# A fused routed-attention and MLP kernel on one core: one pool of eight accumulator banks, 512-column exponentials, steps ordered by a wanted time, weights from the first exponential on, unread matmuls in planned gaps

## The chip, the core and the metric

The kernel runs on one core of a Trainium2 chip. The metric is the time of one launch in device microseconds (us); the figure to beat is the median of three runs. One further execution is profiled, and the traces that are quoted come from that one. The engines are PE (matmuls and transposes; PEld is its weight load), ACT (exponentials, tanh, copies), DVE and POOL (vector work) and SP, which here only issues DMAs. "PEclk" is the TensorE clock that was granted, as a share of full speed.

## The reference

```python
# q, k, v: 4 x 8 x 768 x 64 (batch, head, row, dim); 16 centroids of 64 for each head
q_assign = argmax(q_n . c_n);  k_assign = argmax(k_n . c_n)      # nearest centroid, all normalized
scores = q . k^T / 8, and -1e9 where q_assign != k_assign
attn = softmax(scores);  x = (attn . v), heads side by side      # x: 3072 x 512
h = x @ w_in                                                     # w_in: 512 x 2048
out = (h / (1 + exp(-h))) @ w_out                                # w_out: 2048 x 512
```

Everything comes in and goes out as float32. The mask is made a part of the matmul: each row of q and k gets 16 more numbers, a code of its centroid, so that the 80-row product of a q and a k of different centroids is pushed far down.

## The kernel before

**Tiles.** A batch has 768 rows, which are 6 tiles of 128. A *part* (function `part`) prepares q and k rows of one head or a pair of heads: split float32 into two float16 halves (`hi` L436 or L432, `lo` L440), transpose them (DMA transpose L453, or PE transposes L467 with a copy out of the bank L476/L478), multiply by the centroids (`logits`, L505, or L496 with L500), find the maximum (L532), compare with it (L535, L556, L558), turn the code by 32 x 32 blocks (L565) and place it below the transposed rows in the tile `ab` (four `put`s: DMAs L578, or copies L580 and L582). `attention` then does one head: scores into a bank (L621), the exponential (L634) into the tiles `P`, the product with v (L653), reciprocal and scaling (L666, L671), and for each pair of heads the transpose of the result into `xt` (DMA L690, or PE L701 with copy L708). `mlp` takes a chunk of rows: 16 up blocks of 4 matmuls (L730), tanh (L736), gate (L741), then for each 128 rows 16 down matmuls (L759), a copy out (L772) and the store (L777).

**Stages.** Batch 0 is attended in two goes: first its row tiles 0 and 1 of all 8 heads (called n=0 below), then tiles 2 to 5 (n=1). Then come batches 1, 2 and 3, here b1, b2, b3. The MLP has eight chunks: batch 0 rows 0:2, batch 0 rows 2:6, then two chunks of 3 tiles for each other batch. The prepared rows of batch 0 that n=0 needs go over PE transposes and copies (`twin=True`, `place="ENG"`); the q rows that only n=1 needs, and all of b1 to b3, go over DMA transposes and DMA puts.

**Order.** Nothing is scheduled while the kernel runs: each engine executes a fixed list in order and waits in place. The lists come from `Plan.order`, a planner that is run while the kernel is built: it holds every step with an engine, an assumed duration, the steps that it follows and the buffers that it needs, and always takes the step that can start earliest by its own clock; at equal times the lower `key` wins. Loads and parts of later heads also follow the first exponential of an earlier head (`todo`, `pace`): the first loads of b1 that of head 1 of n=1, in both kernels. Buffers (tiles and PSUM banks) come from pools. The keys before are hand-written numbers: attention head places times 20, MLP steps from 100000 up, and some large negative ones for what should go at once.

**PSUM.** Eight banks of 512 columns: two pairs `pS` for scores only (an exponential reads 768 or 1024 columns of a pair at once), and four single banks `pM` for all else. `exps[-1].adds` gives the four score banks to the second pool after the last exponential.

**Weights.** w_in and w_out come in eight pieces each by POOL's DMA queue (`weight`, L791 and L795). Each step first copies one column of an exponential's result (L789), so that it can't run before that exponential: piece n of w_in hangs on exponential 8 + 2n, piece n of w_out on 26 + 2n, counted over the whole kernel.

**Warm-up.** 60 matmuls of zeros (L278) at the lowest priority keep PE busy before the first real one.

Of the kernel before, what the change touches and what calls it, by code (L numbers as in the profile page):

```python
# [33 lines left out]
class Plan:  # L34
# [33 lines left out]
    def order(self):  # L68
# [12 lines left out]
        done = 0  # L81
        while done < len(self.steps):
            best = None
            for e in engines.values():
# [60 lines left out]
        return sorted(self.steps, key=lambda s: (s.start, s.n))  # L145

@with_exitstack
def kernel(
# [35 lines left out]
    def many(name, n, shape, dt):  # L184
# [21 lines left out]
        "P": (12, [128, 128 * max(NJ, 2 * NB)], f16),  # L206
# [39 lines left out]
    W_IN, W_OUT = 8, 26  # L246
    WARM = 60
    LATE = 1000


    def consts_v():
        nc.vector.memset(zeros, 0.0)
# [21 lines left out]
    def warm(last):  # L274
        y = buf("M")

        def f():
            nc.tensor.matmul(banks[y.i][:, 0:256], zeros[:, 0:128], zeros, start=True, stop=True)  # L278

        return step("PE", 112, f, after=[s_const, last], use=[y], key=1e9, lag=0)  # L280

    last = None
    for _ in range(WARM):
        last = warm(last)
# [41 lines left out]
    def load_v(b, p, key, pace=None):  # L326
# [6 lines left out]
        for h in range(2):  # L333
# [9 lines left out]
            cast_v[b, 2 * p + h] = step("POOL", pool_w(384), g, after=[s, s_ones], use=[x, y], key=key + 60)  # L343
# [47 lines left out]
    def part(b, p, segs, a0, key, hi_eng="POOL", turn="DMA", twin=False, sub="POOL", place="DMA", code_eng=None, pace=None):  # L391

        n = sum(j1 - j0 for _, _, j0, j1 in segs)
# [18 lines left out]
        for kind, h, j0, j1, t, hs in merged:  # L412
# [34 lines left out]
            los.append(step("DVE", dve_w(64 * m, 1.25), lo, after=[x, lds], use=[nat, hl], key=key + 0.1))  # L447

        if turn == "DMA":
# [5 lines left out]
            turned = [step("SP", 120 * n, turn_dma, after=[his, los], use=[hl, A], key=key + 0.5, load=195 * n, flip=True, slack=LATE)]  # L455
        else:
            turned = []
            for kind, h, j0, j1, t, hs in merged:
# [49 lines left out]
        s_log = step("PE", SMALL * n * (2 if twin else 1), logits, after=[turned, s_cent], use=[A, Lb], key=key + 1)  # L508
# [395 lines left out]
```

## Time and profile before

| | before |
|---|---|
| median of 3 runs | 346.21 us (345.95 to 349.98) |
| the profiled execution | 343.36 us, of which its span is 341.5 us |
| PE busy | 310.4 us of the span (91%), mean granted clock 0.95 |
| ACT busy | 224.3 us (66%) |
| DVE busy | 199.0 us (58%) |
| POOL busy | 80.0 us (23%) |
| moved by DMA | 43.88 MB |

The profiled execution has 1.86 us around its span. The median run is 2.85 us above the profiled execution. Busy shares are means over stages that differ much, so the stages are what to read.

### The profile page before, as it was taken

The numbers are of one execution on the slowest core, as the hardware profiler recorded it, in microseconds if no ns is written. First come the engines' busy times: TensorE is split into PE (matmuls) and PEld (weight loads), VectorE is DVE, ScalarE is ACT, GpSimd is POOL, SyncE is SP. The second block draws the span as 40 slices with busy tenths as digits, with TensorE's granted clock in tenths as the row PEclk, the third lists the DMA queues.
The fourth block names the chain that finished last, engine by engine and source line by source line (L and its number), as shares of the span: only waits on it lengthen the run. The fifth ranks groups of instructions, "written<-read, shape, count | busy, mean of one in ns | idle before, by whom it ended". The sixth has DMA issues, their size and how long they took to land.

```text
span 341.5 us, 7888 instructions
## 1 busy us (share of the span) xinstructions
PE 310.4 (91%) x3035; PEld 189.6 (56%) x3035; DVE 199.0 (58%) x467; ACT 224.3 (66%) x359; POOL 80.0 (23%) x168
## 2 busy tenths in 40 slices
PE   8779587796999999979999989999999999989995
PEld 7667454543355555546665656656765564544542
DVE  5988753445465757476975579468873163261430
ACT  4687488563299877687877878768976863351431
POOL 3723441572130233313212214223100000000000
PEclk9955999659899999999999999999999999999999
DMA  7535969999965969888274975996061200101001
GB/s 227 192 111 93 161 94 177 239 166 143 222 127 133 197 135 170 217 203 219 45 136 90 228 192 88 238 209 143 11 121 42 86 2 31 61 2 61 32 30 65
DMA packets 97174, 43.88 MB, mean 128 GB/s; under 512 B 74608, under 2 KB 94064, under 8 KB 97136
## 3 DMA queue, kind: packets, MB, share of 16 engines
q1 hardware_dynamic: 90448, 39.08, 51.6%
q0 software_dynamic: 6400, 4.20, 9.8%
q8 instruction: 24, 0.39, 0.5%
q10 hardware_dynamic: 288, 0.10, 0.1%
q14 instruction: 14, 0.11, 0.1%
HBM read 27.30 MB, written 6.29 MB: 98 GB/s over the span
## 4 chain that ended last, share of the span: by engine, by line
PE 67%; DMA 14%; DVE 6%; ACT 4%; issue 4%; SPq 3%; POOL 1%; ACTq 0%; DVEq 0%; POOLq 0%
PE pM L759 19%; PE pM L730 16%; PE pS L621 14%; DMA ab<-hl 9%; PE pM L653 8%; DMA ab<-ohT 4%; PE pS L730 4%; ACT P L634 2%; SPq L578 2%; PE pS L759 2%; PE pM L505 2%; ACT tn L736 2%; DMA nk<-in_k_dram 2%; PE pM L278 2%; DVE hl L440 1%
## 5 line engine op out<-in xcount | busy, mean ns | idle before, releaser
L634 ACT ACTIVATE P<-pS 128x768 f16<-128x768 f32 (+1 forms) x184 | 149.0, 844 | 43.8 <-PE pS L621 40.4
L621 PE MATMUL pS<-ab 80*128 80x512 f16 (+1 forms) x384 | 90.9, 347 | 8.7 <-DMA ab<-ohT 4.1
L759 PE MATMUL pM<-wout_s,gq 128*128 128x512 f16 x352 | 86.3, 384 | 0.0
L730 PE MATMUL pM<-xt,win_s 128*128 128x384 f16 (+2 forms) x428 | 81.6, 329 | 4.3 <-DMA win_s<-in_moe_w_in_dram 3.7
L741 DVE SCALAR_TENSOR_TENSOR gq<-tn,pM 128x384 f16<-128x384 f32 (+2 forms) x107 | 56.5, 547 | 33.8 <-ACT tn L736 32.6
L730 PEld LDWEIGHTS <-win_s 128*128 128x128 f16 x512 | 49.1, 97 | 42.7 <-issue 5.4
L736 ACT ACTIVATE tn<-pM 128x384 f32<-128x384 f32 (+2 forms) x107 | 51.9, 504 | 20.6 <-PE pM L730 19.6
L759 PEld LDWEIGHTS <-gq 128*128 128x128 f16 x384 | 37.3, 98 | 41.1 <-issue 2.8
L621 PEld LDWEIGHTS <-ab 80*128 80x128 f16 x384 | 35.9, 102 | 34.8 <-issue 12.5
L653 PEld LDWEIGHTS <-P 128*128 128x128 f16 x1152 | 43.9, 102 | 10.5 <-ACT P L634 3.2
L653 PE MATMUL pM<-vt,P 128*128 128x65 f16 x1116 | 45.4, 200 | 2.5 <-ACT P L634 2.1
L535 POOL TENSOR_TENSOR Df<-L,mx 128x192 f32<-128x192 f32 (+1 forms) x28 | 15.1, 541 | 81.5 <-DVE mx L532 80.2
L338 POOL CAST vt<-nv 128x384 f16<-128x384 f32 x32 | 16.6, 543 | 54.4 <-DMA nv<-in_v_dram 32.6
L666 DVE RECIPROCAL rz<-pM 128x6 f32<-128x6 f32 (+2 forms) x39 | 7.1, 182 | 35.3 <-PE pM L653 35.0
L772 ACT COPY ot<-pM 128x512 f32<-128x512 f32 x22 | 12.9, 588 | 22.1 <-PE pM L759 21.4
L741 DVE SCALAR_TENSOR_TENSOR gq<-tn,pS 128x384 f16<-128x384 f32 x21 | 11.6, 554 | 19.6 <-ACT tn L736 16.0
L521 DVE TENSOR_REDUCE L<-pM 128x192 f32<-128x384 f32 (+1 forms) x28 | 14.9, 533 | 13.9 <-PE pM L505 11.3
L440 DVE SCALAR_TENSOR_TENSOR hl<-nq,hl 128x384 f16<-128x384 f32 (+3 forms) x33 | 19.4, 587 | 5.5 <-POOL hl L436 4.4
L440 DVE SCALAR_TENSOR_TENSOR hl<-nk,hl 128x384 f16<-128x384 f32 (+1 forms) x29 | 19.4, 667 | 4.6 <-POOL hl L436 4.6
L736 ACT ACTIVATE tn<-pS 128x384 f32<-128x384 f32 x21 | 9.9, 489 | 14.4 <-DVE gq L741 8.4
L671 DVE TENSOR_TENSOR xn<-pM,rz 128x384 f16<-128x384 f32 (+2 forms) x39 | 18.5, 475 | 1.2
L565 DVE STREAM_TRANSPOSE ohT<-oh 128x384 f16<-128x384 f16 (+2 forms) x33 | 18.6, 565 | 1.0
(59 smaller groups left out, 206.8 us busy)
## 6 DMA issues: line engine op xcount, KB each, us to landing
nv<-in_v_dram SPq DMA_DIRECT2D x16, 384.0 KB, 5.2
out_dram<-ot SPq DMA_DIRECT2D x24, 256.0 KB, 2.2
nk<-in_k_dram SPq DMA_DIRECT2D x15, 384.0 KB, 4.7
nq<-in_q_dram SPq DMA_DIRECT2D x12, 384.0 KB, 4.7
win_s<-in_moe_w_in_dram POOLq DMA_DIRECT2D x8, 256.0 KB, 4.9
wout_s<-in_moe_w_out_dram POOLq DMA_DIRECT2D x8, 256.0 KB, 8.6
ab<-ohT SPq DMA_DIRECT2D x96, 12.0 KB, 1.9
nq<-in_q_dram SPq DMA_DIRECT2D x4, 256.0 KB, 3.9
```

What stands on the lines that cost most here:

```text
L338: nc.gpsimd.tensor_copy(T["vt"][y.i][:, 0 : NJ * VW].rearrange("p (j c) -> p j c", c=VW)[:, :, 0:D], T["nv"][x.i][:, h, :].rearrange("p (j ...
L440: nc.vector.scalar_tensor_tensor(out=dl, in0=src, scalar=QS, in1=dh, op0=ALU.mult, op1=ALU.subtract)
L535: (nc.gpsimd if sub == "POOL" else nc.vector).tensor_tensor(out=T["Df"][Df.i][:, 0:n, :], in0=Lv(), in1=T["mx"][mx.i][:, 0:n].unsqueeze(2) ...
L565: nc.vector.transpose(T["ohT"][ohT.i][:, 0:n, :].rearrange("p n c -> p (n c)"), T["oh"][oh.i][:, 0:n, :].rearrange("p n c -> p (n c)"),)
L621: nc.tensor.matmul(pS[sb.i][:, at : at + 128 * (c1 - c0)], ab[0:80, kt[per * s + i], :], ab[0:80, qt + c0 : qt + c1, :].rearrange("p n c - ...
L634: nc.scalar.activation(out=dst, in_=src, func=AF.Exp, bias=0.0, scale=ESC)
L653: nc.tensor.matmul(banks[O.i][:, (D + 1) * t : (D + 1) * t + nn], w, vt[:, VW * j : VW * j + nn], start=(j == 0), stop=(j == NJ - 1), skip ...
L671: nc.vector.tensor_tensor(out=T["xn"][xn.i][:, 0:nq, (h % 2) * D : (h % 2) * D + D], in0=banks[O.i][:, 0 : (D + 1) * nq].rearrange("p (t c ...
L730: nc.tensor.matmul(banks[bank.i][:, 0:n], win_s[:, r, ts(fb, 128)], T["xt"][xtb[b].i][:, r, 128 * j0 : 128 * j1], start=(r == 0), stop=(r ...
L736: nc.scalar.activation(out=T["tn"][tn.i][:, 0:n], in_=banks[bank.i][:, 0:n], func=AF.Tanh, bias=0.0, scale=1.0)
L741: nc.vector.scalar_tensor_tensor(out=T["gq"][g.i][:, fb % 4, 0:n], in0=T["tn"][tn.i][:, 0:n], scalar=1.0, in1=banks[bank.i][:, 0:n], op0=A ...
L759: nc.tensor.matmul(banks[bank.i], T["gq"][gqs[quarter].i][:, fc % 4, ts(t, 128)], wout_s[:, fc, :], start=(fc == 0), stop=(fc == NFB - 1),)
```

## The change

One pool of eight banks serves all PSUM users, and every exponential reads one bank of 512 columns: for two k tiles of a full head that is 4 q tiles of the first, 4 of the second, and the last 2 of both together (9 exponentials for a head in place of 6 of 768 columns; n=1: 6 of 512 in place of 3 of 1024; n=0: 3 of 512 in place of 2 of 768; 288 in all in place of 184). The matmuls of the scores stay as they were. There are 20 tiles `P` of 512 columns in place of 12 of 1024. Keys become wanted times in us: the table `AT` gives when n=0, n=1, b1, b2, b3 should begin, `ML` when each MLP chunk should, and every step gets a key around that. The down matmuls are planned 2 at a time in place of 4. The weight pieces hang on exponentials 0 to 7 (w_in) and 10 to 17 (w_out), all of them in n=0. The q rows for n=1 go over PE, ACT and DVE (`**engines`) in place of DMA. The 60 warm-up matmuls go; in their place the planner puts an unread matmul of zeros (L284 of the changed kernel) into each gap of over 112 ns that it foresees on PE in its first 80 us while a bank is free. 140 of them come of it: 76 stand ahead of the first scores of n=0, 58 inside n=0 (12 of them right behind its first scores, 44 in its last third), and six later.

```diff
     def order(self):
+            if s.eng == "PE" and self.filler:
+                pool, w, make, until = self.filler
+                while t - e["t"] > w and e["t"] < until and pool.free and pool.free[0][0] <= e["t"]:
+                    x = Step()
+                    x.eng, x.w, x.fn, x.start, x.key, x.n = "PE", w, make(pool.free[0][1]), e["t"], 1e9, s.n - 0.5
...
+                    extra.append(x)
...
-        "P": (12, [128, 128 * max(NJ, 2 * NB)], f16),
+        "P": (20, [128, 512], f16),
...
-    pS = [ps.tile([128, 1024], f32, name=f"pS{i}") for i in range(2)]
-    pM = [ps.tile([128, 512], f32, name=f"pM{i}") for i in range(4)]
-    pools |= {"S": Pool(2), "M": Pool(4)}
+    banks = [ps.tile([128, 512], f32, name=f"bank{i}") for i in range(8)]
+    pools["M"] = Pool(8)
...
-    W_IN, W_OUT = 8, 26
-    WARM = 60
+    W_IN, W_OUT = 0, 10
+    UNREAD = 80000.0
+    AT = [12, 33, 63, 119, 186, 253]
+    ML = [36, 64, 122, 156, 188, 222, 255, 276, 297]
+    FINE = 2
...
-    def part(b, p, segs, a0, key, hi_eng="POOL", turn="DMA", twin=False, sub="POOL", place="DMA", code_eng=None, pace=None):
+    def part(b, p, segs, a0, due, lead=20.0, hi_eng="POOL", turn="DMA", twin=False, sub="POOL", place="DMA", code_eng=None, pace=None):
+        key = due - lead
...
-    def attention(b, h, j0, j1, key, turn):
+    def attention(b, h, j0, j1, key, per, turn):
-        per = {6: 1, 4: 2, 3: 2, 2: 3}[nq]
+        if nq == 6:
+            units = []
+            for j in range(0, NJ, 2):
+                units += [[(j, 0, 4)], [(j + 1, 0, 4)], [(j, 4, 6), (j + 1, 4, 6)]]
+        elif nq == 2:
+            units = [[(j, 0, 2), (j + 1, 0, 2)] for j in range(0, NJ, 2)]
+        else:
+            units = [[(j, 0, nq)] for j in range(NJ)]
...
-    def mlp(b, j0, j1, base, evac):
+    def mlp(b, j0, j1, t0, t1, evac):
-            kk = 100000 + base + fb
+            kk = t0 + (t1 - t0) * fb * 4.0 * n / whole
...
             lambda s, p=p: part(
-                0, p, [("q", 0, NA, NJ), ("q", 1, NA, NJ)], 2 * (NJ + NA), 40 + 20 * p, hi_eng="POOL", pace=s
+                0, p, [("q", 0, NA, NJ), ("q", 1, NA, NJ)], 2 * (NJ + NA), want[1, 2 * p], lead=15.0, pace=s,
+                turn={"q": "ACT"}, code_eng=["DVE", "DVE", "DVE", "ACT"], **engines,
             ),
...
-        w_in_done.append(weight("in", n, exps[W_IN + 2 * n]))
-        w_out_done.append(weight("out", n, exps[W_OUT + 2 * n]))
-    exps[-1].adds = (pools["M"], [4, 5, 6, 7])
+        w_in_done.append(weight("in", n, exps[W_IN + n]))
+        w_out_done.append(weight("out", n, exps[W_OUT + n]))
```

The changed order at three places. First POOL's list where the weights are issued (L789 or L804 is the wait for an exponential, `hl<-nq` the first step of the q rows for n=1). Before, one stretch of it:

```order
L436 TENSOR_SCALAR hl_86<-nq_81 128x8x64
L789 CAST pace<-P_112 128x1
L791 DMA win_s<-in_moe_w_in_dram 128x4x256
L436 TENSOR_SCALAR hl_87<-nq_82 128x8x64
L789 CAST pace<-P_114 128x1
L791 DMA win_s<-in_moe_w_in_dram 128x4x256
L535 TENSOR_TENSOR Df_134<-L_129,mx_132 128x128
L789 CAST pace<-P_104 128x1
```

In the changed kernel, the end of one unbroken row of 16 weight issues and what follows it:

```order
L804 CAST pace<-P_121 128x1
L810 DMA wout_s<-in_moe_w_out_dram 128x2x512
L442 TENSOR_SCALAR hl_88<-nq_80 128x8x64
L442 TENSOR_SCALAR hl_86<-nq_81 128x8x64
L442 TENSOR_SCALAR hl_87<-nq_82 128x8x64
L442 TENSOR_SCALAR hl_88<-nq_83 128x8x64
L342 CAST vt_102<-nv_84 128x6x64
```

All 16 pieces now stand ahead of the four splits for n=1, where before the two kinds alternated. Next SP's list between the q loads for n=1 and the first loads for b1 (`nk_78` with 128x2x384). Before:

```order
L316 DMA nq_82<-in_q_dram 128x2x256
L453 DMA_TRANSPOSE ab_89<-hl_88 128x8x128
L316 DMA nq_83<-in_q_dram 128x2x256
L453 DMA_TRANSPOSE ab_90<-hl_86 128x8x128
L578 DMA ab_89<-ohT_139 16x8x32 x4
L453 DMA_TRANSPOSE ab_91<-hl_87 128x8x128
L453 DMA_TRANSPOSE ab_92<-hl_88 128x8x128
L578 DMA ab_90<-ohT_137 16x8x32 x4
L578 DMA ab_91<-ohT_138 16x8x32 x4
L301 DMA nk_78<-in_k_dram 128x2x384
L578 DMA ab_92<-ohT_139 16x8x32 x4
```

In the changed kernel:

```order
L320 DMA nq_81<-in_q_dram 128x2x256
L320 DMA nq_82<-in_q_dram 128x2x256
L320 DMA nq_83<-in_q_dram 128x2x256
L305 DMA nk_78<-in_k_dram 128x2x384
L320 DMA nq_80<-in_q_dram 128x2x384
L334 DMA nv_84<-in_v_dram 128x2x384
L702 DMA_TRANSPOSE xt_131<-xn_135 128x4x128
L305 DMA nk_79<-in_k_dram 128x2x384
```

The four transposes and 16 puts of n=1 have left SP's list, and the loads of b1 follow at once. Last ACT's list where n=0 ends and n=1 begins (`P` exponentials, `tn` tanh of the first MLP chunk). Before:

```order
L634 ACTIVATE P_107<-pS_149 128x768
L736 ACTIVATE tn_140<-pM_153 128x256
L736 ACTIVATE tn_141<-pM_151 128x256
L736 ACTIVATE tn_142<-pM_152 128x256
L736 ACTIVATE tn_140<-pM_150 128x256
L634 ACTIVATE P_108<-pS_148 128x1024
```

In the changed kernel:

```order
L644 ACTIVATE P_106<-bank_162 128x512
L749 ACTIVATE tn_148<-bank_162 128x256
L749 ACTIVATE tn_149<-bank_161 128x256
L482 COPY ab_89<-bank_160 128x1024
L482 COPY ab_90<-bank_156 128x1024
L749 ACTIVATE tn_150<-bank_159 128x256
L749 ACTIVATE tn_148<-bank_163 128x256
L749 ACTIVATE tn_149<-bank_158 128x256
L482 COPY ab_91<-bank_162 128x1024
L586 COPY ab_89<-ohT_147 16x8x32
L482 COPY ab_92<-bank_157 128x1024
L644 ACTIVATE P_113<-bank_161 128x512
```

Four copies of 1024 columns and the first of four code copies, which the DMAs did before, now stand on ACT ahead of n=1's first exponential.

More of the change, by code (lines that the diff above doesn't have):

```diff
@@ L144, in order @@
             done += 1
-        return sorted(self.steps, key=lambda s: (s.start, s.n))
+        return sorted(self.steps + extra, key=lambda s: (s.start, s.n))
 @with_exitstack
@@ L255, in consts_v @@
         nc.vector.memset(stk, 0.0)
-    s_const = step("DVE", 900, consts_v, key=-100)
+    step("PE", 1, lambda: None, after=[step("DVE", 220, lambda: nc.vector.memset(zeros, 0.0), key=-101)], key=-100)
+    s_const = step("DVE", 700, consts_v, key=-100)
     def consts_p():
@@ L271, with unread @@
     s_ones = [v_ones(i) for i in range(sizes["vt"][0])]
-    def warm(last):
-        y = buf("M")
+    def unread(i):
         def f():
[L278 to L284, printed above, removed]
+            nc.tensor.matmul(banks[i][:, 0:256], zeros[:, 0:128], zeros, start=True, stop=True)
+        return f
+    plan.filler = (pools["M"], 112.0, unread, UNREAD)
     nks, nqs, nvs = {}, {}, {}
@@ L446, in part @@
             his.append(x)
-            los.append(step("DVE", dve_w(64 * m, 1.25), lo, after=[x, lds], use=[nat, hl], key=key + 0.1))
+            los.append(step("DVE", dve_w(64 * m, 1.25), lo, after=[x, lds], use=[nat, hl], key=key + span))
         if turn == "DMA":
@@ L453, in turn_dma @@
                 nc.sync.dma_start_transpose(T["ab"][A.i][:, a0 : a0 + n, :], src)
-            turned = [step("SP", 120 * n, turn_dma, after=[his, los], use=[hl, A], key=key + 0.5, load=195 * n, flip=True, slack=LATE)]
+            turned = [step("SP", 120 * n, turn_dma, after=[his, los], use=[hl, A], key=key + 2 * span, load=195 * n, flip=True, slack=LATE)]
         else:
@@ L506, in logits @@
                     t += 1
-        s_log = step("PE", SMALL * n * (2 if twin else 1), logits, after=[turned, s_cent], use=[A, Lb], key=key + 1)
+        s_log = step("PE", SMALL * n * (2 if twin else 1), logits, after=[turned, s_cent], use=[A, Lb], key=key + 8 * span)
         mx, Df, oh, ohT = buf("mx"), buf("Df"), buf("oh"), buf("ohT")
@@ L527, in Lv @@
                 return T["L"][Lu.i][:, 0:n, :]
-            top = [step("DVE", dve_w(32 * n), total, after=[s_log], use=[Lb, Lu], key=key + 1.2)]
+            top = [step("DVE", dve_w(32 * n), total, after=[s_log], use=[Lb, Lu], key=key + 9 * span)]
         def peak():
@@ L538, in below @@
             )
-        x = step("DVE", dve_w(16 * n), peak, after=top, use=[Lu, mx], key=key + 1.3)
-        s_below = step(sub, pool_w(16 * n, 2.7) if sub == "POOL" else dve_w(16 * n), below, after=[x], use=[Lu, mx, Df], key=key + 1.4)
+        x = step("DVE", dve_w(16 * n), peak, after=top, use=[Lu, mx], key=key + 10 * span)
+        s_below = step(sub, pool_w(16 * n, 2.7) if sub == "POOL" else dve_w(16 * n), below, after=[x], use=[Lu, mx, Df], key=key + 10.5 * span)
         marks = []
@@ L560, in part @@
             marks.append(
[L561 removed]
+                step("DVE", dve_w(16 * (t1_ - t0_), 0.65, 170), mark, after=[s_below, s_const], use=[Df, oh], key=key + 11 * span)
             )
@@ L568, in flip @@
             )
-        s_flip = step("DVE", dve_w(32 * n, 1.04, 180), flip, after=marks, use=[oh, ohT], key=key + 1.6)
+        s_flip = step("DVE", dve_w(32 * n, 1.04, 180), flip, after=marks, use=[oh, ohT], key=key + 12 * span)
         placed = []
@@ L779, in store @@
                 )
-            x = step(eng, act_w(512) if eng == "ACT" else dve_w(512), leave, after=[last], use=[bank, ot], key=-500)
-            step("SP", ISSUE, store, after=[x], use=[ot], key=-500, load=760)
+            x = step(eng, act_w(512) if eng == "ACT" else dve_w(512), leave, after=[last], use=[bank, ot], key=kk - 3)
+            step("SP", ISSUE, store, after=[x], use=[ot], key=kk - 3, load=760)
     def weight(kind, n, x):
```

163 lines of the change are left out of this document (84 added, 79 removed).

## The prediction

> **What bounds the kernel now.** I read the page's shares first, then the 40 slices, then busy time by stage, then the chain.
>
> ```profile
> PE 310.4 (91%) x3035; PEld 189.6 (56%) x3035; DVE 199.0 (58%) x467; ACT 224.3 (66%) x359; POOL 80.0 (23%) x168
> PEclk9955999659899999999999999999999999999999
> DMA  7535969999965969888274975996061200101001
> ```
>
> PE is the busiest by far, but its clock and the DMA share change after slice 10 (85 us). So I cut the span where the program's stages change: the first exponential (16.00), the first up matmul (38.97), the up matmuls of chunk 0, 2:6 (85.84), the first scores of b1 (about 94.5), the end of attention, the last matmul. The last four rows are the stretches at half clock and the window ahead of the first. Columns are busy us of PE, PEld, DVE, ACT, POOL, then the granted clock and the DMA share.
>
> ```profile
> 0.00:16.00 16.00, 13.35 (x175) 11.34 (x175) 11.81 (x36) 7.93 (x15) 9.64 (x30) 1.00 0.66 208
> 16.00:38.97 22.97, 18.89 (x247) 14.96 (x247) 19.25 (x56) 18.11 (x25) 8.23 (x15) 0.63 0.59 120
> 38.97:85.84 46.87, 36.10 (x384) 22.54 (x380) 23.42 (x64) 28.61 (x40) 18.93 (x39) 0.85 1.18 165
> 85.84:94.50 8.66, 8.07 (x31) 3.21 (x30) 4.21 (x9) 2.56 (x5) 1.47 (x3) 0.82 0.97 205
> 94.50:276.00 181.50, 175.42 (x1870) 107.22 (x1868) 117.93 (x262) 143.43 (x227) 41.77 (x81) 1.00 0.65 142
> 276.00:337.80 61.80, 58.53 (x342) 30.33 (x339) 22.34 (x44) 23.09 (x49) 0.00 (x0) 1.00 0.09 35
> 337.80:341.50 3.70, 0.00 (x0) 0.00 (x0) 0.00 (x0) 0.58 (x1) 0.00 (x0) 1.00 0.19 73
> 13.94:17.35 3.41, 2.70 (x52) 2.19 (x52) 3.20 (x8) 3.11 (x6) 2.00 (x5) 1.00 0.37 113
> 17.35:34.42 17.07, 15.20 (x195) 12.46 (x195) 14.37 (x41) 14.38 (x21) 5.21 (x10) 0.50 0.41 96
> 61.73:75.38 13.65, 12.76 (x94) 6.84 (x93) 6.86 (x16) 9.26 (x11) 9.39 (x19) 0.50 1.29 219
> 85.62:89.03 3.41, 3.41 (x17) 1.19 (x14) 1.68 (x5) 0.60 (x1) 0.51 (x1) 0.50 1.14 305
> ```
>
> From 94.5 to 337.8 PE is idle for only 243.3 - 175.42 - 58.53 = 9.4 us, at full clock: nothing but less work for PE could shorten that much. Ahead of it is the slack: between 38.97 and 85.84 (n=1) PE is busy 36.10 of 46.87 us at 0.85 clock, some 30.7 us of work, and DMA is overcommitted at 1.18. The chain names what ended n=1:
>
> ```profile
> 72.78 12.54 DMA ab<-hl
> 85.31 0.05 issue
> 85.36 0.48 PE pM L505 x12
> 85.84 1.71 PE pM L730 x4
> 327.42 10.37 PE pM L759 x48
> ```
>
> A transpose for b1 landed 12.54 us late, PE stood in order behind it, and from 85.84 the rest runs to 327.42 + 10.37 = 337.79. So the time is **T**, where chunk 0, 2:6 starts, plus a nearly full PE list. I work out T, then the list.
>
> **Up to the end of n=0.** The price of a 512-column exponential isn't in the trace; its neighbours are:
>
> ```profile
> L634 ACT ACTIVATE P<-pS 128x768 f16<-128x768 f32 x160 | 125.1, 817 | 34.4 <-PE pS L621 34.1
> L634 ACT ACTIVATE P<-pS 128x1024 f16<-128x1024 f32 x24 | 24.0, 1024 | 9.4 <-PE pS L621 6.3 <-POOL hl L436 2.9
> L772 ACT COPY ot<-pM 128x512 f32<-128x512 f32 x22 | 12.9, 588 | 22.1 <-PE pM L759 21.4 <-ACT P L634 0.5
> 78.57 1.94 ACT L634 ACTIVATE P<-pS 128x1024 f16<-128x1024 f32 x2 [0.94 <-PE pS L621]
> L278 PE MATMUL pM<-zeros 128*128 128x256 f16 x60 | 8.4, 303 | 1.0 <-DVE zeros L252 1.0
> ```
>
> 256 columns more cost 207 ns, so 512 cost 817 - 207 = 610 alone (the copy of that shape: 588). Two in a row take 1.94 in place of 2.05, so about 0.10 is saved when ACT isn't waiting: 0.51 to 0.61, and I take 0.56. n=0 gets 24 of them for 16 of 768: 24 x 0.610 - 16 x 0.817 = +1.6 us on ACT, which is busy 18.11 of 22.97 there. Unread matmuls: 76 now stand ahead of the first scores (60 before) and 12 right behind; at 8.4 / 60 = 0.14 each that is 28 more, up to 3.9 us. PE idles 16.00 - 13.35 = 2.65 us there, which hides most; but eight of them stand ahead of the centroids' transpose (42 in place of 34), and those I count in full: +1.1. The 44 in n=0's last third fall where ACT and DVE set the pace. Against that, PE ran at half clock from 17.35 to 34.42 and was busy 15.20 of 17.07: there it held ACT up. With the clock kept, I return 2.7 of ACT's 4.9 idle us, so the three cancel and the first up matmul stays at **39.0**. Bounds: -4.9 (all of ACT's idle time) to +5.5 (1.6 + 3.9). The 16 weight pieces hide beside this on POOL, which is busy only 8.23 of 22.97; were they late, the q splits behind them would be, and n=1 with them.
>
> **n=0 to n=1.** The q rows for n=1 now take engines: a DVE `lo`, 8 PE transposes, an ACT copy of 1024, 16 logits, three short DVE steps, the block transpose, three copies.
>
> ```profile
> L440 DVE SCALAR_TENSOR_TENSOR hl<-nq,hl 128x512 f16<-128x512 f32 x4 | 2.7, 686 | 0.1
> L476 ACT COPY ab<-pM 128x1024 f16<-128x1024 f16 x3 | 3.0, 1015 | 1.1 <-PE pM L467 1.1
> L535 DVE TENSOR_TENSOR Df<-pM,mx 128x128 f32<-128x128 f32 x2 | 0.6, 292 | 0.1
> L565 DVE STREAM_TRANSPOSE ohT<-oh 128x256 f16<-128x256 f16 x6 | 2.7, 444 | 0.2
> L582 DVE COPY ab<-ohT 16x256 f16<-16x256 f16 x4 | 1.6, 389 | 0.2
> 43.39 1.02 ACT L634 ACTIVATE P<-pS 128x1024 f16<-128x1024 f32 x1 [2.09 <-PE pS L621]
> ```
>
> 0.69 + 1.02 + 3 x 0.29 + 0.44 + 3 x 0.39 = 4.2, with about 1.5 of PE and hand-overs 5.7: n=1's first exponential at 44.7, 1.3 later than the 43.39 of before. Bounds 43.4 (it hides beside n=0's end) to 47 (the first two parts in a row on DVE).
>
> **n=1.** Up to the last n=1 exponential ACT's list holds 48 exponentials of 512, 11 tanh, 3 code copies and 2 copies of 512.
>
> ```profile
> L736 ACT ACTIVATE tn<-pM 128x256 f32<-128x256 f32 x16 | 6.0, 387 | 5.2 <-PE pM L730 4.8
> L580 ACT COPY ab<-ohT 16x256 f16<-16x256 f16 x4 | 1.6, 401 | 1.5 <-DVE ohT L565 1.5
> 83.01 0.42 DVE L708 COPY xt<-pM 128x512 f16<-128x512 f16 x1
> ```
>
> 48 x 0.56 + 11 x 0.39 + 3 x 0.40 + 2 x 0.59 = 33.6: the last one ends at 78.3. PE's 30.7 us and 16 down matmuls more (3.5) fit beside it. Bounds: 0.51 each gives 75.9, 0.61 gives 80.7. Then the last product with v, reciprocal, scaling, transposes and copy (before, from 78.57 + 1.94 = 80.51 to 83.01 + 0.42 = 83.43, so 2.9): 2.1 with less on DVE's queue, so **T = 80.4**.
>
> This needs b1's parts in time. Before, they were late because everything wanted DMA at once:
>
> ```profile
> 42.43 7.81 SPq L578 DMA_DIRECT2D ab<-ohT  x8
> 50.28 0.59 SPq L301 DMA_DIRECT2D nk<-in_k_dram  x1
> 96.21 0.75 POOL L795 DMA_DIRECT2D wout_s<-in_moe_w_out_dram  x1 [0.27 <-issue]
> q0 software_dynamic: 6400, 4.20, 9.8%
> ```
>
> Eight puts for n=1 held SP's queue until 50.24 (7.81 us), b1's first load went at 50.28, and the last weight piece was issued at 96.21. q0, the weights, takes 9.8% of 341.5 = 33.5 us of all 16 engines, 2.1 us a piece. Twelve pieces of 16 lay in n=1 and after, 25 us; DMA's 1.18 x 46.87 = 55.3 us of work there falls to about 30, 0.64 of the time. The pieces now come from 16.5 on and fill the 41% that 16 to 39 left free and some 16 us more. b1's first load, tied to head 1 of n=1, should go near 49 and its codes be placed 23 us later, at about 72, by the loads' 5, the splits' 3, a transpose of 5, 4 on DVE and POOL, 6 for the puts (estimates from the stages of before, less its waits). That is 6 us of cover; beyond that each us late is a us on T.
>
> **Behind T.** The list is that of before from 85.84, less 16 down matmuls (10.37 / 48 = 0.216 each, 3.5) and 12 score matmuls already issued (1.9), less the half clock from 85.62 to 89.03 (1.7): 251.95 - 7.1 = 244.9. On ACT, 211 exponentials stand in that list; 216 of 0.56 in place of 144 of 0.817 are +3 us for b1 to b3, at 0.61 +14, where ACT is busy 143.43 of 181.5: hidden by PE's own list, and if PE ever waited for ACT instead, 14 is the price. Bank waits in one shared pool I take as nothing, by the nearest row, the 75 blocks that already shared four banks with all else:
>
> ```profile
> L730 PE MATMUL pM<-xt,win_s 128*128 128x384 f16 x300 | 56.0, 326 | 0.1
> L730 PE MATMUL pS<-xt,win_s 128*128 128x384 f16 x84 | 15.3, 326 | 3.1 <-ACT tn L736 3.1
> ```
>
> 0.1 us in all. The second row bounds it: 3.1 / 21 = 0.15 us a block; below, 3 us of score waits could go. Down matmuls by twos, 20 tiles `P` and w_out's earlier start cost PE nothing: the same matmuls.
>
> Sum: 80.4 + 244.9 = 325.3; 3.7 for the last copy and store: a span of 329.0, 12.5 less. With the 1.86 around the span 330.9, and the median run lies 2.85 above its profile: **333.7 us**.
>
> **A rule against the change.** In the window 13.94 to 17.35 PE was busy 2.70 of 3.41 us, much of it transposes, and the clock still halved behind it. The Trainium skill, TensorE: Matmul & The Clock Gate, Part 4, says that PE transposes don't count as busy for the clock. The trace agrees that a busy share isn't enough, though it doesn't separate transposes from short matmuls. By that rule the clock would fall in the changed kernel too, since between the 12 unread matmuls behind the first scores and n=0's last third only two stand, among 32 transposes of prepared rows, and the 2.7 above would be lost.
>
> **Rivals.**
> - *The unread matmuls don't keep the clock.* For: only two in n=0's middle, and n=1 has six. Then n=0 ends 2.7 later (336.4), and a second fall like that from 61.73 adds half of 12.76, 6.4 (342.8). Middle 339. Chance 0.18.
> - *b1's parts are late again.* DMA is full from 16 to about 55, and SP still puts codes in order. Then T is 85.84 as before, with before's idle time behind it: 85.84 + 251.95 - 5.4 + 3.7 + 1.86 + 2.85 = 340.8. Against: 25 us of DMA work have left n=1. Chance 0.17.
> - *Slower: bank waits.* PE's list is fixed, and with one pool a score step can land on the bank of an MLP block whose tanh is late; all of PE then waits. Behind T, 112 up blocks and 211 score steps take banks; at 0.15 each it is +48. It decides from 0.06 each, 19.4 us, which gives 353.1; half of the bound gives 358. Chance 0.09.
> - *My forecast*, 333.7, chance 0.56, its own range 320 to 342: ACT at 0.51, all of its idle time in n=0 returned and half of PE's 9.4 idle us gone would be 4.9 + 2.4 + 4.7 less, 321.7.
>
> Range 318 to 346: it takes in the first two rivals and leaves out most of the third and some 0.08 on the fast side. A change within 2% (339.3 to 353.1) is about what can't be told from none. Faster by over 2%: 0.53 of my case, 0.1 of the first rival, 0.07 of the second, 0.70; slower 0.09; the rest 0.21.
>
> **What would show it.** First up matmul near 39, first exponential of n=1 near 45, first up matmul with 512 columns near 80, exponentials of 512 at 0.5 to 0.6, clock 1.0 from 17 on, weights issued by 38, b1's first load near 49, no DMA wait of 12 us ahead of T, PE idle about 10 us behind it. Wrong would be: T at 85 or more, the idle time of PE behind T grown by more than 10 us, or `bank` waits at the head of PE's waits.

## The result, and the profile after

The changed kernel takes 329.9 us in the median of four runs (327.95 to 332.73) against 347.26 in the median of four for the kernel before: a ratio of 0.950, 95% interval 0.939 to 0.960. Measured a second time beside 11 runs of the kernel before it gave 328.3 us and 0.938 (0.932 to 0.944). The forecast was 333.7. Medians below are over all runs of a kernel and ratios over those within 1.5% of its fastest, which in the kernel with both DMA edits undone are two of six, so that its median and its ratio tell different things. The profiled execution took 327.95 us with a span of 326.2.

The page's shares and slices of the changed kernel, to be read against those of before:

```profile
PE 312.1 (96%) x3179; PEld 197.5 (61%) x3179; DVE 201.8 (62%) x479; ACT 239.3 (73%) x471; POOL 75.3 (23%) x164
PEclk9997798999999999999999999999999999999999
DMA  7589990288757869589459469857545011001101
```

PE's idle time, span less busy, was 341.5 - 310.4 = 31.1 us and is now 14.1. The DMA row has moved too: its run of 9s, five slices from 51 to 94 us before, is now three from 24 to 49 us, and the two slices behind it are nearly empty. Busy time by stage, cut at the same events: first exponential (17.40), first up matmul (43.65), n=1's first exponential (50.84), T (86.42), last matmul (322.25); columns as before.

```profile
17.40:43.65 26.25, 21.78 (x298) 18.51 (x295) 16.36 (x49) 18.12 (x33) 17.93 (x38) 0.80 1.26 223
43.65:50.84 7.19, 6.63 (x112) 6.00 (x110) 6.51 (x17) 5.86 (x11) 2.34 (x5) 1.00 0.54 143
50.84:86.42 35.58, 34.57 (x381) 21.02 (x380) 24.66 (x72) 32.88 (x70) 6.13 (x12) 0.95 0.53 114
86.42:322.25 235.83, 232.72 (x2212) 138.07 (x2209) 143.38 (x308) 173.89 (x345) 39.87 (x81) 1.00 0.54 119
```

From the first up matmul to T, PE was idle 46.87 - 36.10 = 10.8 us before and is idle 0.56 + 1.01 = 1.6 now. Behind T it was idle 9.9 and is idle 3.1. But T itself is 86.42, no earlier than the 85.84 of before: the forecast's total came out, its two halves did not.

PE's waits, whole span, first of before, then of the changed kernel (engine, line, what it waited for: us, times, longest):

```profile
PE pS L621 <- DMA ab<-ohT: 4.1, 3, 1.9
PE pM L505 <- DMA ab<-hl: 3.7, 5, 2.4
PE pM L730 <- DMA win_s<-in_moe_w_in_dram: 3.7, 3, 2.5
PE pS L730 <- ACT tn L736: 3.1, 4, 0.8
```

```profile
PE bank L637 <- ACT P L644: 1.9, 1, 1.9
PE bank L713 <- DVE xn L683: 1.5, 2, 0.9
PE bank L637 <- DVE ab L588: 1.4, 1, 1.4
...
PE bank L637 <- DMA ab<-ohT: 1.0, 2, 0.9
...
PE bank L511 <- DMA ab<-hl: 0.5, 1, 0.5
```

Three DMA waits of 11.5 us in all stood at the head; two of 1.5 us are left. Of the 10.8 us of before in n=1, 8.0 were such waits, and the weights themselves came first:

```profile
PE pM L730 <- DMA win_s<-in_moe_w_in_dram: 3.7, 3, 2.5
PE pM L505 <- DMA ab<-hl: 2.4, 1, 2.4
PE pS L621 <- DMA ab<-ohT: 1.9, 1, 1.9
```

So the 12.54 us in the chain of before are the way of that transpose from issue to landing; PE stood for 2.4 us of them.

### The profile page after: what moved, and what is told of

It is laid out like the page before. It is cut to its first block, busy times and chain, and to the rows that moved or that the text cites. A ratio compares the mean times of both kernels' runs of the same rounds, so it can differ in the third digit from the quotient of the medians.

```text
span 326.2 us, 8274 instructions
## 1 busy us (share of the span) xinstructions
PE 312.1 (96%) x3179; PEld 197.5 (61%) x3179; DVE 201.8 (62%) x479; ACT 239.3 (73%) x471; POOL 75.3 (23%) x164
## 4 chain that ended last, share of the span: by engine, by line
PE 79%; DMA 6%; ACT 5%; DVE 5%; issue 2%; SPq 2%; POOL 0%; DVEq 0%; ACTq 0%; POOLq 0%
PE bank L743 24%; PE bank L773 23%; PE bank L637 17%; PE bank L665 10%; ACT P L644 3%; DMA nq<-in_q_dram 3%; PE bank L511 2%; PE bank L284 2%; DMA ab<-hl 2%; DMA ab<-ohT 2%; SPq L584 1%; ACT ab L482 1%; ACT ab L586 1%; PE bank L473 1%; DVE hl L446 1%
## 5 line engine op out<-in xcount | busy, mean ns | idle before, releaser
L644 ACT ACTIVATE P<-bank 128x512 f16<-128x512 f32 x288 | 158.2, 610 | 25.1 <-PE bank L637 23.3
L637 PE MATMUL bank<-ab 80*128 80x256 f16 (+1 forms) x384 | 99.0, 332 | 5.5 <-ACT P L644 1.9
L773 PE MATMUL bank<-wout_s,gq 128*128 128x512 f16 x384 | 100.0, 378 | 0.0
L743 PE MATMUL bank<-xt,win_s 128*128 128x384 f16 (+2 forms) x512 | 96.5, 326 | 0.5 <-DVE xt L720 0.5
L754 DVE SCALAR_TENSOR_TENSOR gq<-tn,bank 128x384 f16<-128x384 f32 (+2 forms) x128 | 69.1, 549 | 28.7 <-ACT tn L749 24.7
L749 ACT ACTIVATE tn<-bank 128x384 f32<-128x384 f32 (+2 forms) x128 | 63.0, 497 | 19.3 <-PE bank L743 18.1
L665 PE MATMUL bank<-vt,P 128*128 128x65 f16 x1152 | 55.0, 196 | 0.6 <-ACT P L644 0.4
L541 POOL TENSOR_TENSOR Df<-L,mx 128x192 f32<-128x192 f32 x24 | 12.7, 530 | 99.5 <-DVE mx L538 99.5
L787 ACT COPY ot<-bank 128x512 f32<-128x512 f32 x24 | 14.1, 586 | 25.7 <-PE bank L773 25.2
L284 PE MATMUL bank<-zeros 128*128 128x256 f16 x140 | 21.7, 312 | 1.0 <-DVE zeros L264 1.0
L683 DVE TENSOR_TENSOR xn<-bank,rz 128x384 f16<-128x384 f32 (+2 forms) x40 | 19.1, 478 | 1.4
L527 DVE TENSOR_REDUCE L<-bank 128x192 f32<-128x384 f32 x24 | 13.3, 554 | 10.6 <-PE bank L511 6.7
L284 PEld LDWEIGHTS <-zeros 128*128 128x128 f16 x140 | 15.0, 112 | 4.3 <-DVE zeros L264 1.0
```

Of the source, the lines that this page charges most:

```text
L284: nc.tensor.matmul(banks[i][:, 0:256], zeros[:, 0:128], zeros, start=True, stop=True)
L637: nc.tensor.matmul(banks[sb.i][:, at : at + 128 * (c1 - c0)], ab[0:80, kt[j], :], ab[0:80, qt + c0 : qt + c1, :].rearrange("p n c -> p (n ...
L644: nc.scalar.activation(out=T["P"][P.i][:, 0:at], in_=banks[sb.i][:, 0:at], func=AF.Exp, bias=0.0, scale=ESC)
L665: nc.tensor.matmul(banks[O.i][:, (D + 1) * t : (D + 1) * t + nn], w, vt[:, VW * j : VW * j + nn], start=(j == 0), stop=(j == NJ - 1), skip ...
L683: nc.vector.tensor_tensor(out=T["xn"][xn.i][:, 0:nq, (h % 2) * D : (h % 2) * D + D], in0=banks[O.i][:, 0 : (D + 1) * nq].rearrange("p (t c ...
L743: nc.tensor.matmul(banks[bank.i][:, 0:n], win_s[:, r, ts(fb, 128)], T["xt"][xtb[b].i][:, r, 128 * j0 : 128 * j1], start=(r == 0), stop=(r ...
```

## The experiments

Four terms make a span comparable: PE's idle time (span less busy), the unread matmuls' busy time, the time at half clock, counted half (span times 1 less granted clock), and the rest. All from each kernel's page:

| kernel | median us | ratio to before | span | idle | unread | half clock costs |
|---|---|---|---|---|---|---|
| before | 347.3 | 1 | 341.5 | 31.1 | 8.4 | 17.1 |
| changed | 329.9 | 0.950 | 326.2 | 14.1 | 21.7 | 6.9 |
| changed, second time | 328.3 | 0.938 | 325.6 | 15.0 | 21.2 | 5.2 |
| unread at the start only, second time | 328.2 | 0.940 | 324.8 | 20.4 | 11.2 | 5.2 |
| weights late | 333.1 | 0.958 | 331.4 | 21.6 | 18.9 | 5.6 |
| MLP behind all | 330.4 | 0.952 | 330.0 | 16.8 | 22.1 | 5.3 |
| pairs of banks | 331.6 | 0.958 | 327.1 | 17.6 | 23.5 | 0 |
| q rows by DMA | 331.8 | 0.953 | 328.8 | 17.1 | 27.5 | 1.6 |
| before + q rows on engines | 345.9 | 0.982 | 341.8 | 33.6 | 8.4 | 10.3 |
| before + early weights + q rows | 330.7 | 0.949 | 328.8 | 23.4 | 9.4 | 6.9 |

From before to changed: idle -17.0, half clock -10.2, unread +13.3, sum -13.9 of the span's -15.3. These terms are an account and no causes: the rest runs from 282.6 to 289.5 us in the table though the other matmuls stay the same, and the half clock can cost less than its term, which counts PE's idle time too: in six runs of the kernel with unread matmuls at the start it went from 5.2 (clock 0.984) to 15.4 (0.953), and the span only from 324.8 to 327.5.

My first theory was that the order by wanted time fills PE and that the unread matmuls only stand in its way.

**Unread matmuls at the start only.**

```diff
-    UNREAD = 80000.0
+    UNREAD = 12000.0
```

> The changed kernel, with the unread matmuls planned only up to 12 us: the 76 ahead of the first scores stay, the 64 in later gaps go; the order of all other steps is planned as in the change. In the changed kernel 16 unread matmuls stand on the chain from 35.16 to 38.05 and 28 more between 39.85 and 43.82, just where the first up matmul came 4.7 us later than forecast. Theory (they stand in PE's way): first up matmul 3 to 5 us earlier, about 39 to 40.5, T (start of chunk 0, 2:6) 3 to 5 earlier too, median about 326. Rival (they keep the clock): without them the half-clock time, 13.65 us in the changed kernel, grows by 7 to 14 us ahead of T, that costs 2.7 to 6 us, and the median is 332 to 336.

Measured: 327.8 us (323.1 to 330.6), ratio 0.937 (0.927 to 0.947). First up matmul at 43.15 in a run with half clock from 22.61 to 46.50, so neither side is clear: half clock grew there by more than the rival forecast, and the median stayed near the theory's 326. The same kernel again, beside the changed one:

> The changed kernel with the unread matmuls planned only up to 12 us (76 in place of 140) once more, beside the changed kernel on the same chip. It is the candidate for a faster version: 327.8 before. Theory (the 64 later ones cost about what the clock that they keep is worth): within 1.5 us of the changed kernel's median either way. Rival (they are dead weight): 2 to 4 us faster.

> The changed kernel as it is, beside the next on the same chip: 328 to 332.

328.24 against 328.29. The group of unread matmuls in this kernel, and the chain of the changed kernel where the later ones stand:

```profile
L284 PE MATMUL bank<-zeros 128*128 128x256 f16 x76 | 11.2, 310 | 1.0 <-DVE zeros L264 1.0
```

```profile
34.49 0.66 PE bank L665 x12
35.16 2.89 PE bank L284 x16
```

They do stand on the chain: without them the first up matmul went at 40.08 instead of 42.73. But what they gain or cost is gone by the end: 10.0 us less of unread matmuls came back as 5.4 more of idle time and 3.8 more in the other matmuls, and 0.8 is left of the span. The theory's small figure (within 1.5) holds. Both profiled executions had a clock of 0.984; over all six runs it was 0.978 with the later ones and 0.966 without them, in the mean, at the same median time. The 64 later ones are neither a cause of the gain nor a loss.

**Fewer at the start.** Until 12 us, planned at 155 ns each:

```diff
-    plan.filler = (pools["M"], 112.0, unread, UNREAD)
+    plan.filler = (pools["M"], 155.0, unread, UNREAD)
```

> The changed kernel, with unread matmuls up to 12 us only and planned at 155 ns each in place of 112 (as the profile shows them, 42 in 7.48 us at the start): 53 instead of 140. In the changed kernel 42 of them ended at 8.52 us, 2.4 us after the centroids were ready for their transpose (on VectorE at 5.77), and the first scores came later. Theory (unread matmuls stand in PE's way, at the start too): the first T copy on ScalarE comes 1.5 to 2.3 us earlier than 9.39, the first exponential 1 us earlier, median 325 to 327. Rival (the early ones bring the clock up sooner or hold it): full clock comes later than 6.7 us or half clock in n=0 grows beyond the 24 us without the later unread matmuls; median 329 to 332.

Measured: 329.1 us, ratio 0.947 (0.940 to 0.953), granted clock 0.942 in the profiled run. The first copy of a transposed row on ACT came at 7.03 for 9.39, as the theory had it, but the half clock's term is 19.1 us there. No gain: the rival's size.

**Weights late.**

```diff
-        w_in_done.append(weight("in", n, exps[W_IN + n]))
-        w_out_done.append(weight("out", n, exps[W_OUT + n]))
+        w_in_done.append(weight("in", n, exps[LATE_IN[n]]))
+        w_out_done.append(weight("out", n, exps[LATE_OUT[n]]))
```

with LATE_IN = [12, 15, 18, 21, 24, 28, 32, 36] and LATE_OUT = [44, 48, 52, 56, 60, 64, 68, 72].

> The changed kernel, with the 16 weight pieces tied to the exponentials at which the kernel before had them (win_s from the middle of n=0 to a third of n=1, wout_s from there to the first head of b1), all else as in the change. Theory (early weights are what keeps DMA free for b1's parts): the DMA share in n=1 goes from 0.53 to over 1, b1's parts come late again, T rises by 3 to 8 us or PE stands idle as long behind it; median 334 to 340. Rival (early weights cost n=0 more than they bring, since DMA's share between the first exponential and the first up matmul rose from 0.59 to 1.26): the first up matmul comes 2 to 4 us earlier and the median is 326 to 329.

Measured: 333.1 us, ratio 0.958 (0.953 to 0.963), and 21.6 us of PE idle. The first two rows of PE's waits are DMA again:

```profile
PE bank L773 <- DMA wout_s<-in_moe_w_out_dram: 5.4, 3, 4.7
PE bank L637 <- DMA ab<-ohT: 3.3, 4, 1.1
```

PE stands behind the weights themselves, in n=1, and behind the codes of later batches. No wait of PE for a transpose of b1's came back, though DMA's share between the first up matmul and T is 1.07. The loss is 3 to 5 us against the two medians of the changed kernel, just under the theory's 334 to 340.

**The MLP behind all else.** Its keys as before:

```diff
-            kk = t0 + (t1 - t0) * fb * 4.0 * n / whole
+            kk = 100000 + t0 + fb
...
-            kk = t0 + (t1 - t0) * (NFB * 4.0 * n + t * NFB * 512.0) / whole
+            kk = 100000 + t0 + 18 + t
```

> The changed kernel, with the MLP's steps planned as before the change: up and down matmuls behind every other step that can go, tanh, gate and copies ahead of all others, in place of a wanted time. Down matmuls stay in twos. Theory (the order by wanted time is what filled PE's idle time behind T, 3.1 us in place of 9.9): the idle time behind T is back, 6 to 8 us, median 336 to 338. Rival (the idle time went because of the pool, the short exponentials and b1's parts in time): within 2 us of the changed kernel, 328 to 332.

Measured: 330.4 us, ratio 0.952 (0.945 to 0.958). The rival's result. The wanted times of the MLP aren't where the idle time went; my first theory falls.

**Pairs of banks.** Two-bank tiles and exponentials of 768 and 1024:

```diff
-                units += [[(j, 0, 4)], [(j + 1, 0, 4)], [(j, 4, 6), (j + 1, 4, 6)]]
+            units = [[(j, 0, 4), (j, 4, 6)] for j in range(NJ)]
...
-            sb, P = buf("M"), buf("P")
+            sb, P = buf("S"), buf("P")
```

> The changed kernel, with PSUM and exponentials as before the change: two tiles of two banks for the scores with exponentials of 768 and 1024 columns, four banks for all else (the other four join after the last exponential), twelve tiles P; weights, wanted times and unread matmuls stay. Theory (the pool and the exponentials' size matter little): ACT gains some 0.08 us per 768 columns, n=0 ends up to 1.6 us earlier, b1 to b3 stay bound by PE; median 328 to 332. Rival (one pool is what lets PE run ahead of ACT, and so what filled the idle time behind T): PE idles 6 us or more longer behind T, waits for P and for pairs head PE's waits, median 336 or more.

Measured: 331.6 us, ratio 0.958 (0.951 to 0.964). Its profiled run never fell to half clock, and still its span is 0.9 us longer. Stage behind T, of this kernel:

```profile
80.68:323.20 242.52, 235.61 (x2208) 138.74 (x2205) 141.54 (x308) 170.99 (x276) 39.36 (x81) 1.00 0.51 116
```

PE is idle 6.9 us behind T, against 3.1 and, in the second profile of the changed kernel, 4.3. So the one pool with short exponentials may hold some 3 us of the idle time behind T, by one or two profiles of each; 3 us are 0.9%, which the ratios can't confirm.

So no part undone alone costs more than 0.8 points of ratio by the first measurement of the changed kernel (0.950), or 2.0 by the second (0.938). The second theory: the gain is two transfers that no longer meet, weights and prepared rows, and it can be had in the kernel before.

**The two DMA edits in the kernel before.** Early weights alone:

```diff
-        w_in_done.append(weight("in", n, exps[W_IN + 2 * n]))
-        w_out_done.append(weight("out", n, exps[W_OUT + 2 * n]))
+        w_in_done.append(weight("in", n, exps[EARLY_IN[n]]))
+        w_out_done.append(weight("out", n, exps[EARLY_OUT[n]]))
```

with EARLY_IN = [0, 1, 1, 2, 3, 3, 4, 5] and EARLY_OUT = [7, 7, 8, 9, 9, 10, 11, 11]; and the q rows of n=1 on engines:

```diff
-                0, p, [("q", 0, NA, NJ), ("q", 1, NA, NJ)], 2 * (NJ + NA), 40 + 20 * p, hi_eng="POOL", pace=s
+                0, p, [("q", 0, NA, NJ), ("q", 1, NA, NJ)], 2 * (NJ + NA), 40 + 20 * p, hi_eng="POOL", pace=s,
+                turn={"q": "ACT"}, code_eng=["DVE", "DVE", "DVE", "ACT"], twin=True, sub="DVE", place="ENG",
```

> The kernel before, with one edit: the 16 weight pieces go from its first exponentials on (win_s at exponentials 0 to 5, wout_s at 7 to 11 of n=0's 16), as early as in the change; all else as before. In the kernel before PE is idle 10.8 us in n=1 and 6.1 us between 94.5 and 276. Theory (the gain is PE's idle time, and the weights' share of it is DMA freed for b1's parts: with late weights in the changed kernel PE was idle 7.6 us more): 5 to 8 us of n=1's idle time go, median 339 to 343. Rival (weights are one of several covers and alone bring nothing, since the eight puts for n=1 still hold SP's queue for 7.8 us ahead of b1's first load): 345 to 348.

> The kernel before, with one edit: n=1's prepared q rows over PE, ACT and DVE; the weights stay late. With early weights alone the kernel before took 340.4, with both edits 330.7. Theory (the two need each other: weights late still fill DMA in n=1, so b1's parts stay late, as DMA's 1.18 share there had it): 341 to 346. Rival (the q rows alone do it, since the eight puts that held SP's queue for 7.8 us ahead of b1's first load are gone): 330 to 334, b1's first load by 45.

> The kernel before, with two edits: the early weights, and n=1's prepared q rows over PE, ACT and DVE in place of DMA transposes and puts; pools, exponentials, planned order and unread matmuls as before. Theory (DMA and SP's queue held b1 back, and both edits together free them): b1's first load goes by about 45, no wait of 12 us for a transpose of b1's, PE's idle time in n=1 falls from 10.8 to under 5, median 335 to 339, that is half or more of the gain of the whole change. Rival (order and pool hold most of the gain): median 341 to 346.

Measured: early weights alone 340.4 us, ratio 0.975 (0.967 to 0.984); q rows alone 345.9, 0.982 (0.975 to 0.989); **both 330.7, 0.949 (0.943 to 0.954)**, better than the theory's 335 to 339: the size of the whole change as first measured, and 1.1 points short of it as measured again. The longest DMA piece in the chain and PE's wait for such pieces, first with early weights alone (profiled in an execution of 344.03 us where the fastest took 337.76, so read for its place and not its size), then with q rows alone:

```profile
34.58 13.67 DMA ab<-hl
PE pM L505 <- DMA ab<-hl: 10.8, 3, 9.3
```

```profile
65.55 16.70 DMA ab<-hl
PE pM L505 <- DMA ab<-hl: 10.0, 5, 5.0
```

Early weights alone take the crowd off n=1 and put it on n=1's q transposes at the end of n=0. Q rows alone leave the late weights where they were, and a transpose for b1 is late in n=1 as before, 16.70 us from issue to landing where it was 12.54. The eight puts ahead of b1's first load aren't what held it: that load went at 16.87, as the rival had it, and the rival's gain didn't come. With both edits PE's waits have no row for these transposes. From issue to landing (least, median, most) those issued between 40 and 95 us took, in before, with q rows alone, with both edits and in the changed kernel:

```profile
DMA to landing us min/median/max: 4.5/10.3/12.5
DMA to landing us min/median/max: 6.1/10.7/16.7
DMA to landing us min/median/max: 3.7/4.1/5.0
DMA to landing us min/median/max: 3.7/4.3/6.5
```

Stages of the kernel with both edits from n=0 (cut at 16.00; its first exponential is at 17.75) to T and behind it, in order:

```profile
16.00:42.38 26.38, 21.06 (x320) 16.05 (x317) 21.80 (x67) 23.34 (x35) 18.60 (x40) 0.82 1.20 228
42.38:81.84 39.46, 36.61 (x427) 24.12 (x426) 25.38 (x73) 32.42 (x48) 7.71 (x15) 0.95 0.59 126
...
81.84:324.61 242.77, 234.88 (x2216) 138.51 (x2213) 139.81 (x308) 166.27 (x275) 41.70 (x81) 1.00 0.49 116
```

DMA's share is 1.20 in n=0 and 0.59 in n=1, nearly the changed kernel's 1.26 and 0.53; PE idles 2.9 us in n=1 in place of 10.8, none of it in a wait for DMA; and the granted clock is that of the changed kernel, 0.979, with the old 60 unread matmuls. From before to this kernel idle time is -7.7, half clock -10.2, unread +1.0 and the rest +4.2, together the span's -12.7: the same total as the whole change, from other terms. Two of the three falls to half clock of before stand behind windows with a DMA wait of PE, 2.45 us for `win_s` in the first and 2.4 for a transpose of b1's in the second:

```profile
58.31:61.73 3.42, 0.97 (x8) 0.69 (x8) 0.24 (x1) 0.84 (x3) 0.79 (x3) 1.00 0.57 114
82.20:85.62 3.42, 0.66 (x14) 0.49 (x15) 1.55 (x5) 0.00 (x0) 0.36 (x1) 1.00 1.26 138
```

Those waits are gone, and the clock between the first up matmul and T is 0.95 for 0.85. That they caused the falls is argued from the order of events and not shown. By the ratios the two edits give 5.1% together and 2.5% and 1.8% apart; the intervals don't exclude a plain sum.

**The same two undone in the changed kernel.** First the q rows by DMA alone:

```diff
                 0, p, [("q", 0, NA, NJ), ("q", 1, NA, NJ)], 2 * (NJ + NA), want[1, 2 * p], lead=15.0, pace=s,
-                turn={"q": "ACT"}, code_eng=["DVE", "DVE", "DVE", "ACT"], **engines,
```

> The changed kernel, with n=1's prepared q rows transposed and put by DMA as before the change, all else as in the change. The plan then has longer gaps for PE before n=1 and fills them: 203 unread matmuls in place of 140. Theory (engines for the q rows keep SP's queue and DMA free for b1): n=1's first exponential comes 1 to 4 us later than 50.8 or b1's parts 3 to 6 late; PE's idle and unread time together grow by 5 us or more, median 334 to 338. Rival (DMA was free enough once the weights went early; the 4.2 us on the engines that end n=0 are saved): median 327 to 331.

Measured: 331.8 us, ratio 0.953 (0.948 to 0.958): between the two, nearer to the rival. Idle and unread time together grew by 8.8 us (17.1 + 27.5 against 14.1 + 21.7), the time by 2 to 3.5, since half clock cost 1.6 in place of 6.9. The theory's late start of n=1 came (54.84 for 50.84), but PE did the first MLP chunk and unread matmuls in that time. The collision that the same DMA rows brought in the old order doesn't come back: PE's longest wait for a transposed tile is 1.3 us here and 9.3 there. Then both edits undone, this one and the late weights above:

> The changed kernel with both undone: weights late, and n=1's q rows by DMA; pool, exponentials, wanted times and unread matmuls stay. Undone singly they gave 333.1 and 331.8, against 329.9. Theory (they are the DMA half of the change and together hold most of the gain, as they did when put into the kernel before): 338 to 344. Rival (order, pool and unread matmuls make a second way to the same gain, so that the two cost their sum at most): 333 to 336.

Measured: runs of 331.0 and 332.2 (ratio 0.949, 0.941 to 0.957) and four between 338.6 and 344.7. The profiled one is that of 332.2 us; from its first up matmul to T:

```profile
43.02:80.52 37.50, 32.46 (x397) 20.97 (x394) 23.30 (x63) 29.30 (x64) 19.30 (x39) 1.00 1.20 207
```

DMA is as crowded there as before (1.20, and 1.18 before), but the transposes take 6.2 in the median from issue to landing in place of 10.3, and PE idles 5.0 us and not 10.8, at full clock. So in this execution pool, order and unread matmuls together are a second way to about the same gain, and the two DMA edits, which are enough for it in the kernel before, weren't needed. No trace shows where the other four lost their time, so whether that way holds stays open.

## Why the prediction was right, and where it wasn't

- **Total and sign**: 333.7 against 329.9, inside the range. The reason at its base, that weights gone from n=1 free DMA for b1's parts, is half of what the two edits in the kernel before show: early weights alone give 2.5%, and with the q rows off DMA 5%. That these two are enough was not in the prediction, which let all edits share the gain.
- **The exponentials**: 610 ns alone, 0.56 in a row. Measured:

```profile
L644 ACT ACTIVATE P<-bank 128x512 f16<-128x512 f32 x288 | 158.2, 610 | 25.1 <-PE bank L637 23.3
L743 PE MATMUL bank<-xt,win_s 128*128 128x384 f16 (+2 forms) x512 | 96.5, 326 | 0.5 <-DVE xt L720 0.5
```

158.2 / 288 = 0.55. **Bank waits** of the up matmuls at nothing: 0.5 us in all, and that for `xt`. The slower rival's price, 0.06 us a block or more, was not there.
- **First up matmul at 39.0**: it was 43.65, within the bounds (-4.9 to +5.5), but the cancelling failed in two of its terms. The unread matmuls ahead of the centroids' transpose cost 2.3 instead of 1.1, by the first copy of a transposed row on ACT (of before, then changed):

```profile
7.07 0.80 ACT L476 COPY ab<-pM 128x768 f16<-128x768 f16 x1 [0.89 <-PE pM L467]
```

```profile
9.39 0.80 ACT L482 COPY ab<-bank 128x768 f16<-128x768 f16 x1 [3.58 <-PE bank L473]
```

  of which 1.4 reached the first exponential (17.40 for 15.99). And the clock, counted as kept for -2.7, was half in n=0 for 10.2 us. ACT idled 26.25 - 18.12 = 8.1 us there instead of 2.2. The later unread matmuls hold 2.7 us of the miss, as the second pair of runs showed (42.73 and 40.08). The half clock in n=0:

```profile
23.72:27.14 3.42, 3.42 (x35) 3.11 (x34) 1.93 (x8) 2.85 (x5) 3.28 (x8) 0.50 1.39 219
30.55:37.38 6.83, 6.17 (x77) 4.95 (x76) 4.25 (x13) 3.99 (x8) 6.55 (x16) 0.50 1.36 201
```

- **"The 16 weight pieces hide on POOL"**: this step failed. On POOL's timeline of the changed kernel, its first and last piece and the split behind them:

```profile
18.41 0.99 POOL L806 DMA_DIRECT2D win_s<-in_moe_w_in_dram  x1
...
36.95 0.71 POOL L810 DMA_DIRECT2D wout_s<-in_moe_w_out_dram  x1
37.69 1.80 POOL L442 TENSOR_SCALAR hl<-nq 128x512 f16<-128x512 f32 x3
```

  and with the weights late:

```profile
19.77 1.23 POOL L442 TENSOR_SCALAR hl<-nq 128x512 f16<-128x512 f32 x2
```

  where 28 exponentials were done by 41.9, so that n=1, which follows on 24, had begun before the first up matmul at 42.52.
  POOL was free enough in sum; but the pieces wait in its queue for exponentials, and the q splits behind them were held to 37.69. I had named that queue and counted its wait as nothing. The hand-over from n=0 to n=1 took 7.2 us instead of 5.7, behind an n=0 already 4.7 late.
- **n=1**: 35.58 us from its first exponential to T against 35.7. Right, with DMA at 0.53 for the 0.64 forecast and no DMA wait of PE from n=1's first exponential to T. But the prediction read the 12.54 us of before as the time for which PE stood; it was 2.4, and the weights it waited for (3.7) weighed more. T was 86.42 for 80.4, all of it brought along from n=0.
- **b1's first load near 49**: wrong. Its k went at 19.00 and its q at 44.26. The tie to head 1 of n=1 is the planner's alone; SP issues as its queue and the buffers allow.
- **Behind T**: 239.8 us to the end of the span against 248.6. I kept PE's idle time there (9.9) as it was; 3.1 are left (4.3 in the second profile). The rest of the miss is PE's work, 232.7 for 244.9 - 9.9 = 235.0. Only the 321.7 case had let some of it go. Where scores keep pairs of banks it is 6.9 in the changed order and 7.9 in the old one with both DMA edits, so by these profiles the pool with short exponentials accounts for some half of the 6.8 that went. The rest was not traced to one edit; the MLP's wanted times aren't it (without them 3.0 behind T, which is at 96.65 there: 229.45 - 226.42 in that kernel's row; 3.6 from 86.42 on).

T mis-sized by +6.0 and the list behind it by -8.8: the two misses cancel to -2.8 of span. That the total is nearer than its terms is luck.

## What to carry to other kernels

When two users of DMA collide, moving one of them can move the collision: look for the next transfer in the new place, and take both off together if it needs that. Before an edit is called hidden on a lightly used engine, list what stands behind it in that engine's queue and what each piece ahead waits for; the busy share says nothing of that. Parts that are worth little when undone singly may still be enough for the gain: put them into the old kernel, one and both, and undo both in the new one, before dropping or crediting any.

## What the hardware showed that I had not expected

The number of unread matmuls alone doesn't set the clock: the mean of the granted clock was 0.949 with 60 of them in the kernel before (11 runs) and 0.978 with the same 60 once both DMA edits were in (4 runs). Within the changed kernel the clock does go with it, 0.978 with 140 (6 runs), 0.966 with 76 (6) and 0.952 with 53 (4), but the median time of the first two was the same.

Of the changed kernel, windows ahead of a fall to half clock (first two, and the fourth), and two at half clock behind which it rose (third and fifth):

```profile
20.31:23.72 3.41, 1.45 (x35) 0.95 (x32) 3.25 (x9) 2.48 (x6) 2.81 (x7) 1.00 1.10 296
27.14:30.55 3.41, 1.99 (x31) 1.75 (x29) 2.06 (x7) 2.84 (x6) 0.32 (x2) 1.00 1.45 196
33.97:37.38 3.41, 3.28 (x26) 2.60 (x27) 2.76 (x9) 1.21 (x2) 3.39 (x9) 0.50 1.27 205
51.03:54.44 3.41, 2.95 (x9) 0.85 (x9) 3.18 (x11) 3.36 (x8) 0.96 (x3) 1.00 0.00 0
54.44:57.86 3.42, 3.37 (x30) 2.05 (x30) 1.77 (x7) 3.00 (x7) 0.00 (x0) 0.50 0.03 5
```

The first, second and fourth make it look as if a thin window were enough for a fall, and the other two as if a full one were needed and enough for a rise. The kernel before has windows that say otherwise; the clock stayed at full behind the first and at half behind the second:

```profile
41.24:44.66 3.42, 1.90 (x19) 1.42 (x20) 0.86 (x3) 1.33 (x4) 0.12 (x1) 1.00 0.84 138
24.18:27.59 3.41, 3.41 (x61) 3.00 (x59) 2.35 (x8) 3.09 (x5) 0.00 (x0) 0.50 0.00 0
```

So no rule on PE's busy share of one window comes out of these traces. The fourth window holds nothing but nine score matmuls of 512 columns at ACT's pace, no transpose, and PE counts as busy 2.95 of 3.41 us; the clock fell all the same. Down matmuls of 512 columns in a row took 0.216 us each (10.37 / 48 in the chain of before), by which nine are 1.9 us, so a count of busy time overstates the work here. The Trainium skill, TensorE: Matmul & The Clock Gate, Part 1, has the clock fall after an idle window of some 3.4 us; here it fell behind windows in which PE was busy for 1.45 to 2.95 us. Its Part 4, which says that PE transposes don't count as busy in the same way, wasn't needed for the fourth.
